# Forming A's value rows inside the first sixteen heads instead of in the lead

## The chip, the cores and the metric

The kernel runs on one core of a Trainium2 chip. Its time is the device time of one execution in microseconds (us). Before the change it was 2752.17 us, the median of three runs (2751.70 to 2752.62). The engines are TensorE (PE: matmuls, with its weight loads shown apart as PEld), VectorE (DVE), ScalarE (ACT), GpSimd (POOL) and SyncE (SP, which here only issues DMAs). Sixteen DMA engines carry all transfers, whichever queue issues them.

## The reference, cut to what matters

Two attention layers read the same `x` (2048 x 576) with 32 heads of width 18. A has its own keys and values for each head; B has one key and one value for all heads. A sigmoid gate mixes them:

```python
x = A_x
g = _sigmoid((x * gate_w).sum(-1, keepdims=True))
a = _A_ref(x, A_wqkv, A_wo)    # softmax(q k^T / sqrt(18)) v, 32 heads with own k and v, then @ wo
b = _B_ref(x, B_wq, B_wk, B_wv, B_wo)    # the same with one k and one v for 32 heads
return g * a + (1 - g) * b
```

Everything is float32. The kernel forms products of activations and weights as sums of three products of a high and a low part (h*h + l*h + h*l).

## The kernel before, in words

B's heads are units 0 to 31 (`u < H`), A's heads units 32 to 63. The program is recorded in order by hand: each engine executes its instructions in the order in which the Python code emits them, and waits come from the tiles that instructions share. There are three stages.

**The projecting stage.** `X["h"]` and `X["l"]` hold x transposed, as a high part (5 blocks of 128 rows) and a low part (4 blocks), in SBUF. All columns that are needed row-wise (B's key, gate, B's value, B's queries, A's queries and keys) are stacked into 14 tiles `mt` of 128 rows. `project(mt, c, w)` forms one quarter (512 columns) of such a tile: 14 matmuls of 512 columns (`products`, L153 of the profile) into a PSUM tile of the pool `ps_s` (three buffers, named ps). `leave` takes it out: ScalarE copies the high part into `phl` (L159; four buffers), VectorE subtracts it for the low part (L165), and a DMA on GpSimd's queue writes both to `qk_d` in DRAM. Where a tile holds keys, its second quarter also yields the difference of the first two key quarters (`pd`, `pdhl`, written to `kd_d`). Tiles 0 to 2 are done while x still arrives; `project_rest` does tiles 3 to 13, 44 quarters, one after another. Between quarters `bring_row` issues one of the loads that bring rows back for the first heads (`ksb`, `kdb`, `qs`: DMAs of 18 rows on SP's queue, which also loads weights `wst` and A's value weights `vwst`).

**The lead.** Scores are exponentiated after subtracting a row maximum, so the maxima run 22 steps ahead (`LEAD = 22`; a step is one block of 128 queries of one unit). Before the main loop, 16 slices form the first maxima. Slice `v` forms two value units, six bank products `step_max` (L412; the first two into `ps_s`, the other four into `ps_m`, which has four buffers) that VectorE reduces (L421). A value unit `project_v(st_, hf, w)` forms A's values of 128 positions for half of the heads: 14 matmuls of 288 columns (L192) into `ps_s`, a copy by ScalarE into `vst` (L195) and a DMA on ScalarE's queue to `v_d` in DRAM, from which each group of four A heads is loaded later (`load_vg`, first at step 482). At slice 11, `max_rows(0)` finishes unit 0's maxima. After the lead `open_ph2` frees X and the weights and opens the pools of the main loop.

**The main loop.** 64 units of 16 steps. A step has four score products (L447), four exponentials on ScalarE (L454), a share of later units' bank products and reduces, and the sums over values (L460). Strings of letters set the order on TensorE: s is a score product, m, x and y are bank products for the maxima, digits are quarters of sums over values, U takes one unit of side work from `todo`.

```python
PLAIN = "sm sy sm 4 sm sm sm 2 sm sx 2"
SPARSE = "sx U sm ys sx 4 sm ms sm 3 ys ms sx 3 sm ms ms 4 sm ms ms 2 ms sy 2 ms ms sx 4 ms sm ys 3 " \
         "ms ms ms 3 sm ms ms 4 sm ms"
```

PLAIN covers two steps without side work. SPARSE covers eight steps and has one U. Before the change it is used at steps 522 to 777, for the 32 units of the first output projection (`out_proj`: 12 matmuls of 288 columns into `ps_m`, L595, and a copy by ScalarE into `oacc`, L598). DENSE and ALONE serve the later parts, which the change does not touch. `when(T, f)` calls f when step T begins; `slow` is a list of generators that get one turn at each second step (gates, normalisation, output weights).

Of the kernel before, what the change touches and what calls it, by code (L numbers as in the profile page):

```python
# [8 lines left out]
F32 = mybir.dt.float32  # L9
# [33 lines left out]
def gated_mix_kernel(ctx: ExitStack, tc: tile.TileContext, xT, wall, wv, wo, out):  # L43
# [21 lines left out]
    sum_d = dram.tile([NU, S], F32, name="sum_d")  # L65
    r_d = dram.tile([NU, S], F32, name="r_d")
    v_d = dram.tile([16, P, H * 19], F32, name="v_d")
    on_d = [dram.tile([9 * P, S], F32, name=f"on{x}") for x in "hl"]


# [85 lines left out]
    def leave(mt, c, fp):  # L156
# [17 lines left out]
        if mt == 0:  # L174
            dma(z_d[cs], st[ROW_G:ROW_G + 1, :])
            return c, st

    def shared_v(c, st):
        pv = ps_m.tile([P, 512], F32, name="pm")
        for j in range(4):  # L180
            nc.tensor.transpose(pv[:, 18 * j:18 * j + 18],
                                st[ROW_VB:ROW_VB + 18, j * P:(j + 1) * P],
                                ident[ROW_VB:ROW_VB + 18, ROW_VB:ROW_VB + 18])
        nc.vector.tensor_copy(vb[:, 4 * c:4 * c + 4, 0:18],
                              pv[:, 0:72].rearrange("p (j d) -> p j d", d=18))

    vst = [stp.tile([P, 16, 19], F32, name=f"vst{i}", bufs=1) for i in range(3)]

    def project_v(st_, hf, w):
        fp = ps_s.tile([P, 512], F32, name="ps")  # L190
        for n, (a, b, k, kr) in enumerate(PROJ):
            nc.tensor.matmul(fp[:, 0:288], X[b][:kr, k, st_ * P:(st_ + 1) * P], w[a][:kr, k, :],  # L192
                             start=(n == 0), stop=(n == len(PROJ) - 1))
        t = vst[st_ % 3]
        nc.scalar.activation(t[:, :, 0:18], fp[:, 0:288].rearrange("p (h d) -> p h d", d=18), AF.Copy)  # L195
        dma(v_d[st_, :, 304 * hf:304 * hf + 304], t.rearrange("p h d -> p (h d)"), nc.scalar)

    def run(gen):
        for _ in gen:
# [9 lines left out]
        if rows_back:  # L209
            rows_back.pop(0)()  # L210

    WV = []
    VS = [None, None]
    with tc.tile_pool(name="xs", bufs=1, side="right") as xsp:
        XS = []

        def load_x(c, rest=None):
            half = c < 2
            XS.append(xsp.tile([P, NKT, 256 if half else 512], F32, name="xsh" if half else "xs", bufs=2))
            load5(XS[c], xT[:, 256 * c:256 * c + 256] if half else xT[:, 512 * (c - 1):512 * c], rest)  # L220

        def main_w(st):

            w = {y: wpool.tile([P, NKT, P], F32R, name=f"w{y}", bufs=3) for y in "hl"}
            nc.scalar.activation(w["h"][:, 0:4], st[:, 0:4], AF.Copy)
            nc.vector.tensor_tensor(w["l"][:, 0:4], st[:, 0:4], w["h"][:, 0:4].bitcast(F32), op=OP.subtract)
            return w

        def last_w(st, w):
            nc.scalar.activation(w["h"][:, 4], st[:, 4], AF.Copy)  # L230
            nc.vector.tensor_tensor(w["l"][:, 4], st[:, 4], w["h"][:, 4].bitcast(F32), op=OP.subtract)

        def split_x(c):
            xs = XS[c // 2 + 1][:, :, 256 * (c % 2):256 * (c % 2) + 256] if c > 1 else XS[c]
            cs = slice(c * 256, (c + 1) * 256)
            nc.scalar.activation(X["h"][:, :, cs], xs, AF.Copy)
            low_x(c, xs)
            last_x(c, xs)

        def low_x(c, xs):  # L240
            cs = slice(c * 256, (c + 1) * 256)
            nc.vector.tensor_tensor(X["l"][:, :, cs], xs[:, 0:4], X["h"][:, 0:4, cs].bitcast(F32), op=OP.subtract)

        def last_x(c, xs):
            xh = X["h"][64:128, 4, c * 256:(c + 1) * 256]
            nc.vector.tensor_tensor(xh, xs[64:128, 4], xh.bitcast(F32), op=OP.subtract)

        W = [load_w(0, nc.scalar)]
        load_x(0, nc.scalar)
        nc.scalar.activation(ones, ones, AF.Copy)  # L250
        W.append(load_w(1, nc.gpsimd))
        W.append(load_w(2, nc.gpsimd))
        load_x(1, nc.gpsimd)

        warm = ps_m.tile([P, 512], F32, name="pm")
        for i in range(6):
            nc.tensor.matmul(warm[:, 0:304], ident, vb.rearrange("p k d -> p (k d)"), start=True, stop=True)
        for c in range(2, 5):
            load_x(c)
        dma(ones_r.rearrange("a (b c) -> (a b) c", c=32), ones)  # L260
        for mt in range(3, 6):
            W.append(load_w(mt))
        for t in vst:
            nc.gpsimd.memset(t, 1.0)

        x0, xh = XS[0], X["h"][:, :, 0:256]
        ST = [W.pop(0) for _ in range(3)]
        WP = [main_w(ST[0])]
        nc.scalar.activation(xh[:, 0:2], x0[:, 0:2], AF.Copy)  # L269
        nc.vector.tensor_copy(xh[:, 2:4], x0[:, 2:4])  # L270
        low_x(0, x0)
        WP.append(main_w(ST[1]))
        WP.append(main_w(ST[2]))
        last_w(ST[0], WP[0])
        nc.scalar.activation(xh[:, 4], x0[:, 4], AF.Copy)
        last_x(0, x0)
        last_w(ST[1], WP[1])
        last_w(ST[2], WP[2])
        split_x(1)
        FP = [ps_s.tile([P, 512], F32, name="ps") for _ in range(3)]  # L280
        for n in ((0, 12), (12, 14)):
            for mt in range(3):
                products(FP[mt], WP[mt], 0, 0, 256, *n)
        for c in range(4):
            for mt in range(3):
                if mt == 2:
                    if c < 3:
                        split_x(2 * c + 2)
                        split_x(2 * c + 3)
                    shared_v(*keep)  # L290
                if c == 0:
                    products(FP[mt], WP[mt], 0, 256, 256)
                    done = leave(mt, c, FP[mt])
                else:
                    done = project(mt, c, WP[mt], 2 if c == 1 and mt == 0 else 1)
                if mt == 0:
                    keep = done
                    if c == 3:
                        WN = prep_w(W.pop(0))
    vwp = ph1.enter_context(tc.tile_pool(name="vwp", bufs=1, side="right"))  # L300

    def load_wv(hf):
        VS[hf] = vwp.tile([P, NKT, 288], F32, name="vwst")
        load5(VS[hf], wv[:, 288 * hf:288 * hf + 288])

    for b in (SB, MB):
        later(ksb[b + 54:b + 56, :], ones_r)
# [2 lines left out]
    for u in range(3):  # L310
        load_q(u, put=later)

    def project_rest(WN):
        for mt in range(3, MT):
            w = WN
            if mt + 1 < MT:
                WN = prep_w(W.pop(0))
            if mt + 3 < MT:
                W.append(load_w(mt + 3))
            if mt == 5:  # L320
                load_wv(0)
            for c in range(4):
                project(mt, c, w)
                bring_row()
            if mt in (8, 11):
                hf = (mt - 8) // 3
                WV.append({y: vwp.tile([P, NKT, 288], F32R, name=f"vw{y}{hf}") for y in "hl"})
                split_w(VS[hf], WV[hf], nc.vector)
                if hf == 0:
                    load_wv(1)  # L330
        assert not rows_back

    project_rest(WN)


    small = ctx.enter_context(tc.tile_pool(name="small", bufs=1, side="left"))
# [32 lines left out]
    def open_ph2():  # L369
        ph1.close()  # L370
        L["pt"] = ctx.enter_context(tc.tile_pool(name="ppool", bufs=14, side="left"))
        L["work"] = ctx.enter_context(tc.tile_pool(name="work", bufs=2, side="left"))
        p2 = ctx.enter_context(tc.tile_pool(name="p2", bufs=1, side="right"))
        L["pool"] = p2
        L["ks"] = [p2.tile([P, S], F32R, name=f"ksa{i}") for i in range(2)] + [ksb]
        L["kds"] = [p2.tile([P, 512], F32R, name="kda"), kdb]
        L["oacc"] = p2.tile([P, 16, D], F32, name="oacc")
        for t in L["ks"][:2]:
            for b in (SB, MB):
                dma(t[b + 54:b + 56, :], ones_r)  # L380

    VG = {}

# [319 lines left out]
    for t in range(8):  # L703
        when(16 * (last_head(t) + 1) + 5, lambda t=t: slow.append(normalise(t)))
    when(16 * (NU - 1) + 2, lambda: run(normalise(8, at_end=True)))
    SEG = ((0, [P] * 4, 450, 518), (4, [P] * 4, 862, 942))
    for t0, rows, Ta, Tb in SEG:
        when(Ta, lambda t0=t0, rows=rows: slow.append(prep_wo(t0, rows)))
# [2 lines left out]
    when(980, load_gates)  # L711


    vunits = [(st_, hf) for hf in range(2) for st_ in range(16)]
    banks = [(M, c) for M in range(LEAD + 2) for c in range(4)]
    for v in range(16):
        if v == 11:
            max_rows(0)
        for st_, hf in vunits[2 * v:2 * v + 2]:
            project_v(st_, hf, WV[hf])  # L720
        for n, (M, c) in enumerate(banks[6 * v:6 * v + 6]):
            step_max(*divmod(M, 16), c, c % 2 == 1, ps_s if n < 2 else ps_m)
        if v >= 4 and slow:
# [64 lines left out]
    while pos["s"] < 4 * NSTEP:  # L788
# [4 lines left out]
            emit(ALONE, 1 if T < 1012 else 0)  # L793
        elif T >= SEG[1][3] + 4:
            emit(DENSE, 1)
        elif SEG[0][3] + 4 <= T < SEG[0][3] + 4 + 8 * 32:
            emit(SPARSE, 1)
        else:
            emit(PLAIN)
# [43 lines left out]
```

## Time and profile before

| what | us |
|---|---|
| median of three runs | 2752.17 |
| the profiled execution, its own time | 2752.82 |
| its span, first to last instruction | 2750.5 |
| TensorE busy | 2741.8 |
| VectorE busy | 2413.1 |
| ScalarE busy | 2432.6 |
| GpSimd busy | 216.8 |
| the lead, from the first value matmul to the first score | 189.85 to 266.37 |

The mean granted clock of TensorE was 0.999. The profile comes as a page (busy times, the span in slices, DMA queues, the chain of work that ended last, the costliest groups of instructions) and as answers from the trace: the chain in order of time, a timeline of single instructions, busy times by stretch, DMA landings. Rows of a timeline give the start, the length, the engine, the line, the operation, what is written and read, the shapes, and how many instructions were merged; a bracket says how long the engine was idle before and who ended that. A matmul's length is modelled and overlaps its successor, so the pace is read from starts. In rows of stretches the columns are busy time of TensorE, weight loads, VectorE, ScalarE and GpSimd with their counts, then the granted clock, the share of the DMA engines and GB/s.

### The profile page before, as it was taken

How to read it: one execution, taken by the hardware profiler on the slowest of the kernel's cores; microseconds unless marked ns; L12 is line 12 of the kernel's file. 1: busy time of each engine (PE TensorE's matmuls, PEld its weight loads, DVE VectorE, ACT ScalarE, POOL GpSimd, SP SyncE). 2: the span in 40 equal slices, each digit the busy share in tenths (PEclk: the TensorE clock that was granted, in tenths of full speed). 3: DMA queues.
4: the chain of work that ended last, by engine and by line, in shares of the span. 5: the costliest groups of instructions: out<-in, count | busy, mean ns of one | idle time of the engine just before them, and what ended most of it. 6: DMA issues, size and time to landing. Idle time of an engine off the chain costs nothing.

```text
span 2750.5 us, 59178 instructions
## 1 busy us (share of the span) xinstructions
PE 2741.8 (100%) x22968; PEld 1264.3 (46%) x22968; DVE 2413.1 (88%) x4521; ACT 2432.6 (88%) x4781; POOL 216.8 (8%) x355
## 2 busy tenths in 40 slices
PE   9999999999999999999999999999999999999999
PEld 7888333333333333333334444444444333334554
DVE  4347999999999999999999898898989999998873
ACT  4322999999999999999999999999999999998776
POOL 2220000001000100100110001000100011011000
PEclk9999999999999999999999999999999999999999
DMA  8752010112102111210133223222321233223312
GB/s 283 271 222 70 25 32 27 33 47 67 31 27 56 52 32 35 63 47 27 53 94 107 84 60 94 93 68 74 102 86 47 67 88 96 67 81 116 111 35 88
DMA packets 123511, 217.24 MB, mean 79 GB/s; under 512 B 53082, under 2 KB 80810, under 8 KB 111544
## 3 DMA queue, kind: packets, MB, share of 16 engines
q1 hardware_dynamic: 107806, 170.79, 20.8%
q0 software_dynamic: 10496, 37.49, 3.6%
q10 hardware_dynamic: 4928, 5.18, 0.5%
q8 instruction: 180, 2.95, 0.5%
q14 instruction: 101, 0.83, 0.1%
HBM read 137.23 MB, written 67.40 MB: 74 GB/s over the span
## 4 chain that ended last, share of the span: by engine, by line
PE 98%; DVE 1%; DMA 1%; SPq 0%; ACT 0%; issue 0%; DVEq 0%; ACTq 0%
PE acc L460 38%; PE ps L447 36%; PE pm L412 9%; PE ps L153 6%; PE pm L595 4%; PE ps L192 2%; DVE mx L421 1%; DMA xsh<-xT 0%; PE pm L447 0%; PE ps L412 0%; DMA R<-r_d 0%; DMA r_d<-sm 0%; SPq L49 0%; DVE oacc L604 0%; DVE junk L418 0%
## 5 line engine op out<-in xcount | busy, mean ns | idle before, releaser
L454 ACT ACTIVATE pt<-ps 128x512 f32<-128x512 f32 x4052 | 2129.9, 611 | 106.6 <-PE pm L412 44.6
L421 DVE TENSOR_REDUCE mx<-pm 128x1 f32<-128x512 f32 x3064 | 1945.7, 683 | 140.3 <-PE pm L412 96.3
L447 PE MATMUL ps<-qs,ksb 56*128 56x512 f32 x2688 | 905.8, 437 | 0.3
L412 PE MATMUL pm<-ksb,qs 54*128 54x512 f32 x2332 | 807.0, 441 | 0.0
L447 PEld LDWEIGHTS ps<-qs,ksb 56*128 56x128 f32 x2688 | 437.2, 184 | 643.1 <-ACT pt L454 618.1
L460 PE MATMUL acc<-pt,vb 128*19 128x256 f32 (+1 forms) x6144 | 592.5, 457 | 0.1
L460 PE MATMUL acc<-pt,vg 128*19 128x256 f32 (+3 forms) x6432 | 573.8, 443 | 0.4 <-DVE oe L472 0.4
L447 PE MATMUL ps<-qs,ksa 56*128 56x512 f32 x1364 | 453.7, 437 | 0.1
L412 PE MATMUL pm<-ksa,qs 54*128 54x512 f32 x1232 | 425.5, 438 | 0.0
L412 PEld LDWEIGHTS pm<-ksb,qs 54*128 54x128 f32 x2332 | 373.8, 184 | 35.1 <-DVE mx L421 15.2
L418 DVE CUSTOM_DVE_ANT_0 junk<-pm,xb 128x512 bf16<-128x512 f32 x500 | 339.7, 679 | 1.0 <-ACT xb L415 0.9
L447 PEld LDWEIGHTS ps<-qs,ksa 56*128 56x128 f32 x1364 | 218.0, 184 | 246.7 <-ACT pt L454 217.6
L415 ACT ACTIVATE xb<-pm 128x512 f32<-128x512 f32 x500 | 305.2, 610 | 0.0
L412 PEld LDWEIGHTS pm<-ksa,qs 54*128 54x128 f32 x1232 | 197.7, 184 | 56.5 <-DVE mx L421 26.0
L460 PEld LDWEIGHTS acc<-pt,vg 128*19 128x19 f32 x6432 | 122.1, 97 | 215.3 <-issue 190.0
L460 PEld LDWEIGHTS acc<-pt,vb 128*19 128x19 f32 x6144 | 104.2, 97 | 210.3 <-issue 200.2
L412 PE MATMUL pm<-kdb,qs 54*128 54x512 f32 x372 | 150.4, 404 | 0.0
L115 POOL CAST mh<-mt 128x32 fp32r<-128x32 f32 x64 | 13.5, 211 | 1726.0 <-DVE mt L429 1725.9
L159 ACT ACTIVATE phl<-ps 128x512 fp32r<-128x512 f32 x56 | 33.5, 599 | 100.8 <-PE ps L153 72.0
L165 DVE TENSOR_TENSOR phl<-ps,phl 128x512 fp32r<-128x512 f32 x56 | 38.7, 691 | 92.0 <-ACT phl L159 69.4
L153 PE MATMUL ps<-xh,wh 128*128 128x512 f32 (+1 forms) x300 | 83.5, 377 | 0.6 <-ACT xh L269 0.6
L153 PE MATMUL ps<-xh,wl 128*128 128x512 f32 (+1 forms) x300 | 83.2, 375 | 0.0
(123 smaller groups left out, 1379.6 us busy)
## 6 DMA issues: line engine op xcount, KB each, us to landing
qs<-qk SPq DMA_DIRECT2D x384, 144.0 KB
qk<-phl POOLq DMA_DIRECT2D x56, 512.0 KB, 4.6
ksa<-qk SPq DMA_DIRECT2D x132, 144.0 KB
ksb<-qk SPq DMA_DIRECT2D x66, 144.0 KB
onh<-oh SPq DMA_DIRECT2D x32, 256.0 KB
onl<-ol SPq DMA_DIRECT2D x32, 256.0 KB
oih<-onh SPq DMA_DIRECT2D x16, 512.0 KB
oil<-onl SPq DMA_DIRECT2D x16, 512.0 KB
```

The costliest lines, as they stand in the source:

```text
L153: nc.tensor.matmul(fp[:, p0:p0 + g], w[a][:kr, k, :], X[b][:kr, k, x0 + p0:x0 + p0 + g], start=(n == 0), stop=(n == len(PROJ) - 1))
L159: nc.scalar.activation(hl[:, 0, :], fp, AF.Copy)
L165: nc.vector.tensor_tensor(hl[:, 1, :], fp, hl[:, 0, :].bitcast(F32), op=OP.subtract)
L192: nc.tensor.matmul(fp[:, 0:288], X[b][:kr, k, st_ * P:(st_ + 1) * P], w[a][:kr, k, :], start=(n == 0), stop=(n == len(PROJ) - 1))
L412: nc.tensor.matmul(pm, qs[u % 3][b:b + 54, i * P:(i + 1) * P], k, start=True, stop=True)
L415: nc.scalar.activation(MX["x", u, i], pm, AF.Relu)
L418: nc.vector.tensor_tensor_reduce(junk, pm, MX.pop(("x", u, i)), 1.0, -3e38, op0=OP.add, op1=OP.max, accum_out=MX[u][:, i, c:c + 1])
L421: nc.vector.tensor_reduce(MX[u][:, i, c:c + 1], pm, axis=AX.X, op=OP.max)
L447: nc.tensor.matmul(ps, kst(u)[b:b + 56, i * P:(i + 1) * P], qs[u % 3][b:b + 56, c * 512:(c + 1) * 512], start=True, stop=True)
L454: nc.scalar.activation(pt, ps, AF.Exp, scale=SCALE)
L460: nc.tensor.matmul(acc[32 * j:32 * j + 19, a:b], v_of(u, i), PT[u, i, j][:, a:b], start=(i == 0), stop=(i == 15), skip_group_check=True)
L595: nc.tensor.matmul(fp[:, 0:288], x, y, start=(n == 0 and not joins), stop=(n == len(ops) - 1))
```

## The change

Three things move.

1. The value units leave the lead. They become a generator `value_units`, whose 32 units are taken one for each SPARSE block of eight steps at steps 10 to 265, in heads 0 to 16. A unit has the same 14 matmuls and the same copy, but into `ps_m`, and its result is stored from SP's queue.
2. By then X has been freed, so its parts go through DRAM: in the projecting stage eight stores (`store_x`, after every third quarter) write X to `x_d`, and the split value weights go to `wv_d` in four stores (`store_wv`), all on GpSimd's queue. The value weights are loaded from the first quarter on, and one set of split buffers serves both halves. In the main loop `value_units` loads the four weight parts once and, for every two units, the 128 columns of X (`xv`, two buffers) on SP's queue. The rows that were brought back over 44 quarters are brought back over 28.
3. The last four tiles of projected rows, mt 10 to 13 (16 quarters), are formed in the lead, one per slice, in place of the two value units. They leave through `leave_lead`: ScalarE copies the PSUM tile twice (plain, and high part), and GpSimd subtracts, in place of VectorE.

The accumulator `oacc` gets its memory after the value units are done (`open_oacc`, step 274).

```diff
+    x_d = dram.tile([P, 2 * NKT - 1, S], F32, name="x_d")
+    wv_d = dram.tile([2, 2, P, NKT * 288], F32, name="wv_d")
...
+    def leave_lead(mt, c, fp):
+        hl = stp.tile([P, 2, 512], F32R, name="phl", bufs=4)
+        st = stp.tile([P, 512], F32, name="pst", bufs=3)
+        nc.scalar.activation(st, fp, AF.Copy)
+        nc.scalar.activation(hl[:, 0, :], fp, AF.Copy)
+        nc.gpsimd.tensor_tensor(hl[:, 1, :], st, hl[:, 0, :].bitcast(F32), op=OP.subtract)
+        dma(qk_d[:, mt * P:(mt + 1) * P, c * 512:(c + 1) * 512].rearrange("a p f -> p a f"), hl, nc.gpsimd)
+        if c == 0:
+            KD[mt] = st
+        if c == 1:
+            d = stp.tile([P, 512], F32, name="pd", bufs=1)
+            nc.gpsimd.tensor_tensor(d, st, KD.pop(mt), op=OP.subtract)
+            dhl = stp.tile([P, 2, 512], F32R, name="pdhl", bufs=1)
+            split(d, dhl[:, 0, :], dhl[:, 1, :], nc.scalar, nc.gpsimd)
+            dma(kd_d[mt * P:(mt + 1) * P, 0:2, :], dhl, nc.gpsimd)
+            dma(kd_d[mt * P:(mt + 1) * P, 2, :], dhl[:, 0, :], nc.gpsimd)
...
+    def store_wv(hf, st):
+        w = {y: vwp.tile([P, NKT, 288], F32R, name=f"vw{y}") for y in "hl"}
+        split_w(st, w, nc.vector)
+        for i, y in enumerate("hl"):
+            dma(wv_d[hf, i], w[y].rearrange("p k f -> p (k f)"), nc.gpsimd)
+
+    def store_x(i):
+        y, c = "hl"[i % 2], i // 2
+        cs = slice(512 * c, 512 * c + 512)
+        dma(x_d[:, 0:NKT, cs] if y == "h" else x_d[:, NKT:, cs], X[y][:, :, cs], nc.gpsimd)
...
+    left = tiles_left(WN)
+    for n in range(4 * (LEAD_T - 3)):
+        mt, c, w = next(left)
+        if n in (0, 10):
+            vs = load_wv(n // 10)
+        project(mt, c, w)
+        bring_row()
+        if c == 3:
+            bring_row()
+        if n in (8, 18):
+            store_wv(n // 10, vs)
+        if n % 3 == 1 and n // 3 < 8:
+            store_x(n // 3)
...
+    def value_units():
+        pool = L["vx"]
+        XV = {}
+        def load(st_):
+            XV[st_] = pool.tile([P, 2 * NKT - 1, P], F32R, name="xv", bufs=2)
+            dma(XV[st_], x_d[:, :, st_ * P:(st_ + 1) * P])
+        load(0)
...
+        yield
+        for st_ in range(16):
+            if st_ < 15:
+                load(st_ + 1)
+            x = XV.pop(st_)
+            for hf in range(2):
+                fp = ps_m.tile([P, 512], F32, name="pm")
+                for n, (a, b, k, kr) in enumerate(PROJ):
+                    nc.tensor.matmul(fp[:, 0:288], x[:kr, k if b == "h" else NKT + k, :], w[hf][a][:kr, k, :],
+                                     start=(n == 0), stop=(n == len(PROJ) - 1))
+                nc.scalar.activation(vst[hf][:, :, 0:18], fp[:, 0:288].rearrange("p (h d) -> p h d", d=18), AF.Copy)
+                dma(v_d[st_, :, 304 * hf:304 * hf + 304], vst[hf].rearrange("p h d -> p (h d)"))
+                yield
...
+    VB = 10
+    when(VB - 8, lambda: (todo.append(value_units()), pull(1)))
+    when(VB + 8 * 32 + 8, open_oacc)
...
-        for st_, hf in vunits[2 * v:2 * v + 2]:
-            project_v(st_, hf, WV[hf])
+        mt, c, w = next(left)
+        fp = ps_s.tile([P, 512], F32, name="ps")
+        products(fp, w, c * 512, 0, 512)
+        leave_lead(mt, c, fp)
...
-        elif SEG[0][3] + 4 <= T < SEG[0][3] + 4 + 8 * 32:
+        elif any(b <= T < b + 8 * 32 for b in (VB, SEG[0][3] + 4)):
             emit(SPARSE, 1)
```

`tiles_left` yields (mt, c, w) for tiles 3 to 13 in the order of `project_rest`, with the same weight loads and splits ahead. Here `LEAD_T` is `MT - 4`, so the loop above forms 28 quarters and the lead the other 16.

More of the change, by code (lines that the diff above doesn't have):

```diff
@@ L185, in shared_v @@
                               pv[:, 0:72].rearrange("p (j d) -> p j d", d=18))
[L187 to L196, printed above, removed]
     def run(gen):
@@ L210, in bring_row @@
             rows_back.pop(0)()
-    WV = []
-    VS = [None, None]
     with tc.tile_pool(name="xs", bufs=1, side="right") as xsp:
@@ L262, in gated_mix_kernel @@
             W.append(load_w(mt))
-        for t in vst:
-            nc.gpsimd.memset(t, 1.0)
         x0, xh = XS[0], X["h"][:, :, 0:256]
@@ L302, in load_wv @@
     def load_wv(hf):
-        VS[hf] = vwp.tile([P, NKT, 288], F32, name="vwst")
-        load5(VS[hf], wv[:, 288 * hf:288 * hf + 288])
+        t = vwp.tile([P, NKT, 288], F32, name="vwst")
+        load5(t, wv[:, 288 * hf:288 * hf + 288])
+        return t
+    def store_wv(hf, st):
[7 more added lines that the diff above has]
+        dma(x_d[:, 0:NKT, cs] if y == "h" else x_d[:, NKT:, cs], X[y][:, :, cs], nc.gpsimd)
     for b in (SB, MB):
@@ L311, in gated_mix_kernel, with tiles_left @@
         load_q(u, put=later)
-    def project_rest(WN):
+    LEAD_T = MT - 4
+    def tiles_left(WN):
         for mt in range(3, MT):
@@ L319, in project_rest @@
                 W.append(load_w(mt + 3))
-            if mt == 5:
-                load_wv(0)
             for c in range(4):
[L323 to L333, printed above, removed]
+                yield mt, c, w
+    left = tiles_left(WN)
[11 more added lines that the diff above has]
+            store_x(n // 3)
+    assert not rows_back
     small = ctx.enter_context(tc.tile_pool(name="small", bufs=1, side="left"))
@@ L376, in open_ph2 @@
         L["kds"] = [p2.tile([P, 512], F32R, name="kda"), kdb]
-        L["oacc"] = p2.tile([P, 16, D], F32, name="oacc")
+        L["early"] = ExitStack()
+        L["vx"] = L["early"].enter_context(tc.tile_pool(name="vx", bufs=1, side="right"))
         for t in L["ks"][:2]:
@@ L380, in open_ph2, with open_oacc @@
                 dma(t[b + 54:b + 56, :], ones_r)
+    def open_oacc():
+        L["early"].close()
+        L["oacc"] = ctx.enter_context(tc.tile_pool(name="oacc", bufs=1, side="right")) \
+            .tile([P, 16, D], F32, name="oacc")
+    def value_units():
[5 more added lines that the diff above has]
+        load(0)
+        w = [{y: pool.tile([P, NKT, 288], F32R, name=f"vw{y}{hf}") for y in "hl"} for hf in range(2)]
+        for hf in range(2):
+            for i, y in enumerate("hl"):
+                dma(w[hf][y], wv_d[hf, i].rearrange("p (k f) -> p k f", k=NKT))
+        vst = [pool.tile([P, 16, 19], F32, name=f"vst{i}") for i in range(2)]
+        for t in vst:
+            nc.gpsimd.memset(t, 1.0)
+        yield
[3 more added lines that the diff above has]
+            x = XV.pop(st_)
+            for hf in range(2):
+                fp = ps_m.tile([P, 512], F32, name="pm")
[5 more added lines that the diff above has]
+                yield
     VG = {}
@@ L711, in gated_mix_kernel @@
     when(980, load_gates)
-    vunits = [(st_, hf) for hf in range(2) for st_ in range(16)]
     banks = [(M, c) for M in range(LEAD + 2) for c in range(4)]
```

## The prediction

> **What bounds the kernel now.** I read the page first (busy time, the chain that ended last), then the chain in order of time, then single stretches.
>
> ```profile
> PE 2741.8 (100%) x22968; PEld 1264.3 (46%) x22968; DVE 2413.1 (88%) x4521; ACT 2432.6 (88%) x4781; POOL 216.8 (8%) x355
> ...
> PE 98%; DVE 1%; DMA 1%; SPq 0%; ACT 0%; issue 0%; DVEq 0%; ACTq 0%
> ```
>
> TensorE is busy all the time and carries 98% of the chain. The change removes no matmul; it moves matmuls between three stretches, so its worth is the difference of what they cost there, plus whatever new wait makes TensorE stop. The chain in order of time gives the price in each:
>
> ```profile
> 46.96 143.05 PE ps L153 x630
> 190.01 3.71 PE ps L192 x28
> ...
> 261.73 3.90 PE ps L192 x28
> ...
> 311.20 1.05 PE acc L460 x8
> 348.23 1.05 PE acc L460 x8
> ...
> 1478.42 1.78 PE pm L595 x12
> ...
> 2093.59 1.79 PE pm L595 x12
> ```
>
> Columns are start, length, what, and how many matmuls. The projecting stage runs 630 matmuls, 45 tiles of 14, in 143.05 us: 3.179 us a tile. The lead's slices follow each other every (261.73 - 190.01) / 15 = 4.78 us. A head of 16 plain steps takes 348.23 - 311.20 = 37.03 us, so 8 steps 18.52. Eight steps with one unit of the first output projection, the SPARSE pattern, take (2093.59 - 1478.42) / 31 = 19.84.
>
> **The change, part by part.**
>
> *Tiles out of the projecting stage.* Sixteen leave: 16 x 3.179 = 50.9 us saved, all on the path.
>
> *Value units into heads 0 to 16.* A projection unit has 12 matmuls of 288 columns, a value unit 14.
>
> ```profile
> 1577.55 0.79 PE L595 MATMUL pm<-woh,oih 128*128 128x288 f32 x4
> ...
> 1578.19 0.69 PE L595 MATMUL pm<-woh,oil 128*128 128x288 f32 x4
> ...
> 1578.72 0.69 PE L595 MATMUL pm<-wol,oih 128*128 128x288 f32 x4
> ...
> 1579.34 0.18 PEld L447 LDWEIGHTS ps<-qs,ksa 56*128 56x128 f32 x1 [0.16 <-ACT xb L415]
> ```
>
> Four start 0.53 us apart, so one takes 0.133. A unit of 12 costs 19.84 - 18.52 = 1.33 us over plain steps (the SPARSE order returns part of it), one of 14 costs 1.59. 32 x 1.59 = 51.0 us added. The other engines do not bind there:
>
> ```profile
> 311.00:348.00 37.00, 37.00 (x322) 14.05 (x320) 35.58 (x68) 36.33 (x73) 0.47 (x2) 1.00 0.11 31
> ...
> 1478.40:1637.20 158.80, 158.80 (x1506) 77.26 (x1505) 140.75 (x267) 149.63 (x295) 1.86 (x8) 1.00 0.25 75
> ```
>
> Columns: TensorE, weight loads, VectorE, ScalarE, GpSimd, granted clock, DMA share, GB/s. ScalarE falls from 98% in plain steps to 94% beside units; the value unit's eviction (128x288) has the shape of the projection unit's. The loads of X parts, 576 KB every 16 steps, and the stores of 152 KB, now on SP's queue instead of ACT's, meet a DMA share of 0.11: nothing. What stands behind the store on SP are row loads for two or three heads ahead, nothing that a 2 us wait makes late. If the cover were gone, each late load would stop TensorE for its own landing.
>
> *Start of the units.* Xv and four weight parts, 576 + 4 x 720 KB = 3.5 MB, are issued after the lead and needed at step 10, some 22 us after it. At 315 GB/s (SP's rate, below) they take 11 us, after up to 7 us for the last writes of the lead whose memory they take. Cost 0; late at most 3 us.
>
> *The lead.* Products move from 28 matmuls of 288 columns a slice to 14 of 512.
>
> ```profile
> 256.87 0.79 PE L192 MATMUL ps<-vwh,xh 128*128 128x288 f32 x4
> ...
> 260.55 0.29 PE L192 MATMUL ps<-vwl,xh 128*128 128x288 f32 x1
> 260.77 0.50 PE L412 MATMUL ps<-ksb,qs 54*128 54x512 f32 x2
> ...
> 261.31 1.29 DVE L421 TENSOR_REDUCE mx<-ps 128x1 f32<-128x512 f32 x2 [1.12 <-PE ps L412]
> ...
> 261.67 0.80 PE L192 MATMUL ps<-vwh,xh 128*128 128x288 f32 x4
> ```
>
> ```profile
> L117 POOL TENSOR_TENSOR ol<-ot,oh 128x512 fp32r<-128x512 f32 x32 | 41.2, 1286 | 6.9 <-DMA onl<-ol 4.9
> ...
> L49 POOL DMA_DIRECT2D qk<-phl x56 | 40.6, 726 | 123.2 <-DVE phl L165 117.5 <-issue 3.6 <-DVE vb L184 2.0
> ...
> L159 ACT ACTIVATE phl<-ps 128x512 fp32r<-128x512 f32 x56 | 33.5, 599 | 100.8 <-PE ps L153 72.0 <-issue 26.6 <-ACT wh L125 1.3
> ...
> L421 DVE TENSOR_REDUCE mx<-ps 128x1 f32<-128x512 f32 x32 | 20.6, 686 | 18.9 <-PE ps L412 18.9
> ...
> L126 DVE TENSOR_TENSOR wl<-wst,wh 128x640 fp32r<-128x640 f32 x11 | 9.1, 825 | 0.0
> L125 ACT ACTIVATE wh<-wst 128x640 fp32r<-128x640 f32 x11 | 8.0, 731 | 0.0
> ```
>
> These are groups: count | busy us, mean ns of one | idle before. Products take 260.77 - 256.87 = 3.90 us, 28 x 0.133 = 3.71 of it streaming and 0.19 the switch; the six bank products 0.90. With TensorE alone the new slice is 3.18 + 0.19 + 0.90 = 4.27. But three tiles a slice now come out of the three buffers ps where there were four, and in the built order the products of most slices take the buffer that the first bank product of the slice before held. Its reduce starts at 261.31, 0.54 after the product, and lasts 0.69; with 0.16 for TensorE to go on, as after xb in the rows of the unit, it resumes 1.39 after the first bank product, not 0.90. Slice: 3.18 + 0.19 + 1.39 = 4.76, sixteen of them 0.3 us below before. Where a slice takes the buffer of the products before it, ScalarE's two copies are waited for, and at c = 1 ScalarE itself waits for GpSimd (subtract, issue, subtract). Two copies of 0.60 delay three slices by some 0.35 us; 2 x 1.29 + 0.73 = 3.3 us before the split at c = 1 delays one by 0.9: together +2. GpSimd's own load, six subtractions and six issues or 12 us in four slices of 19, is hidden; so are three weight splits that come along (0.73 on ScalarE, 0.83 on VectorE, which has 4.76 - 6 x 0.69 = 0.6 to spare a slice). Lead: +1.7, between -8.2 (all slices 4.27) and +5 (ScalarE's copies waited for in each).
>
> *New traffic in the projecting stage.* This is the term that decides. X goes out in eight stores (1280 or 1024 KB), the split value weights in four of 720 KB, all on GpSimd's queue between the writes of projected rows.
>
> ```profile
> q0 software_dynamic: 8415, 30.42, 56.1%
> q1 hardware_dynamic: 4506, 7.52, 16.7%
> ...
> qk<-phl POOLq DMA_DIRECT2D x45, 512.0 KB, 4.3
> kd<-pdhl POOLq DMA_DIRECT2D x9, 512.0 KB, 4.0
> ...
> kd<-pdhl POOLq DMA_DIRECT2D x9, 256.0 KB, 4.1
> ```
>
> These are the DMA view's rows for 47 to 190 us: packets, MB, share of 16 engines; then issues with KB and us to landing. GpSimd's queue moves 30.42 MB in 56.1% of 143 us, 379 GB/s of full share; SP's 7.52 MB in 16.7%, 315 GB/s. In the 22 tiles from the first X store to the last (69.9 us of TensorE), the new queue holds 22 x 512 + 4 x 768 + 9216 + 2880 KB = 27.1 MB, SP's 22/28 of 7.52 = 5.9 MB. At those rates that is 71.4 + 18.8 = 90.2 us of all engines. The densest stretch shows how far the engines go:
>
> ```profile
> 28.00:40.00 12.00, 12.00 (x56) 9.68 (x55) 7.19 (x10) 6.01 (x8) 3.36 (x5) 1.00 1.04 403
> 60.00:80.00 20.00, 20.00 (x90) 16.57 (x89) 5.68 (x8) 5.80 (x10) 4.35 (x6) 1.00 0.93 327
> 95.00:120.00 25.00, 25.00 (x112) 20.71 (x111) 9.63 (x14) 8.19 (x14) 8.03 (x12) 1.00 0.61 231
> ```
>
> ```profile
> DMA to landing us min/median/max: 7.2/8.0/8.3
> ```
>
> ```profile
> DMA to landing us min/median/max: 3.1/3.2/4.9
> ```
>
> The last two are the landings of qk writes issued from 60 to 80 us and from 95 to 120, where SP's queue is empty.
>
> The share reaches 1.04 for 12 us, so 90.2 / 1.04 = 86.7 us: 16.8 more than TensorE needs. Some of it is hidden. Each tile's copy waits for the write four tiles earlier (phl has four buffers), issued 1.7 us after that tile, so 4 x 3.18 - 1.6 = 11.1 us may pass; three PSUM buffers let TensorE run on for 4.9 more. A landing may take 16 us before TensorE stops. From 60 to 80 us, where SP's row loads run beside the writes, it already takes 8.0. So 8 us are left and 16.8 - 8 = 8.8 us of stall remain. Ends: at the 403 GB/s of the first row 33.0 MB take 81.9 us, a stall of 4.0; with neither the 1.04 nor any slack 20.3. I take 8.8, since the row with both queues at work measures the same loads. A store of 640 pieces is issued by GpSimd in 0.73 us or a few times that, beside some 2 us of idle time a tile.
>
> The Trainium skill, HBM Reference, Specifications, says a core streaming alone reaches about 425 GB/s; by that 33.0 MB would take 77.6 us and the slack would hide all of the excess, an estimate. The rows here reach 403.
>
> **Sum:** -50.9 + 51.0 + 1.7 + 8.8 = +10.6 us. The profiled execution took 2752.82 us, 0.65 over the median 2752.17; against the median: 2762.8.
>
> A stop long enough also costs clock:
>
> ```profile
> 265.00:270.00 5.00, 4.70 (x19) 2.47 (x18) 3.68 (x6) 3.62 (x8) 0.00 (x0) 0.91 0.20 70
> 270.00:275.00 5.00, 5.00 (x20) 2.21 (x21) 2.12 (x5) 3.16 (x8) 0.00 (x0) 0.50 0.02 7
> 275.00:280.00 5.00, 5.00 (x40) 1.56 (x38) 4.36 (x8) 4.46 (x9) 0.00 (x0) 0.91 0.00 0
> ```
>
> Where scores wait for exponentials the granted clock falls to 0.50; (0.09 + 0.50 + 0.09) x 5 = 3.4 us of clock are lost. In a stretch bound by transfers that is free, at its end it may add up to 3.4.
>
> **The rivals.**
>
> 1. *Transfers keep up* (not slower). Place: the 22 tiles. It decides from 33.0 MB / (69.9 + 8) = 424 GB/s on. For: 403 was held beside small loads, and the stores are large. Against: landings of 8.0 us at a share of 0.93. Time: 2762.8 - 8.8 = 2754.
> 2. *The lead runs at TensorE's pace*, 4.27 a slice: -8.2 in place of +1.7. For: VectorE has time to spare in each slice. Against: the buffer order. Time: 2753 with the stall, 2744 where rival 1 holds too, the one way to be faster by over 0.2%.
> 3. *The stall is longer*: no slack, 20.3 us, a cold clock at its end (+3.4). For: SP's loads of 18 rows come closer together, and lengthened landings from 3.2 to 8.0. Time: 2762.8 + 11.5 + 3.4 = 2778.
>
> **How the numbers follow.** Forecast 0.50, own range 2758 to 2770. Rival 1 alone 0.18, rival 2 with the stall 0.08, both together 0.08, rival 3 0.16. The range leaves out half of rival 3 and rivals 1 and 2 together: 2748 to 2775. Within 0.2% of 2752.17 (2746.7 to 2757.7, about what a measurement of this kernel can tell from no change) lie rival 1 but for 0.03 with lead slices in between, rival 2 with the stall, and 0.03 of the forecast's with a stall near 4: 0.15 + 0.08 + 0.03 = 0.26. Faster: 0.08 + 0.03 = 0.11. Slower: 0.47 + 0.16 = 0.63.
>
> **What would show it.** Right: in the profile after, the projecting stage's 28 later tiles take about 98 us instead of 89, with ScalarE's copies into phl waiting for DMA, the share of the engines near 1.0 and landings of 12 to 17 us; lead slices of 4.7 to 4.8 us whose products wait for VectorE's reduce; heads 0 to 16 at 20.1 us per 8 steps. Wrong: no TensorE gap before the lead; lead slices near 4.3; a gap at the first unit; or units that cost under 1.3 or over 1.9 us.

## The result and the profile after

The changed kernel takes 2762.76 us (median of six runs, 2761.49 to 2763.48), the kernel before in the same runs 2752.11: a ratio of 1.0039, 95% interval 1.0026 to 1.0052. The prediction was 2762.8. The profiled execution of the changed kernel took 2762.81 us with a span of 2761.0, against 2752.82 and 2750.5 before.

First the page of the changed kernel: busy time, and the engines' shares of the chain that ended last.

```profile
PE 2738.1 (99%) x23480; PEld 1296.8 (47%) x23480; DVE 2394.6 (87%) x4497; ACT 2443.7 (89%) x4793; POOL 256.7 (9%) x390
...
PE 96%; DMA 2%; DVE 1%; ACT 0%; issue 0%; POOL 0%; ACTq 0%; POOLq 0%
```

TensorE's share of the chain fell from 98% to 96%; that of transfers rose from 1% to 2%, and the chain has a row that it did not have before, the writes of projected rows (`DMA qk<-phl`, 1.6%). The chain in order of time (start, length, what, how many) shows where they are:

```profile
47.47 31.99 PE ps L155 x140
...
94.34 15.19 DMA qk<-phl
...
113.35 15.79 DMA qk<-phl
...
129.67 14.14 DMA qk<-phl
...
164.90 3.44 PE ps L155 x14
...
220.79 3.44 PE ps L155 x14
...
250.55 2.04 PE pm L437 x14
...
873.59 2.08 PE pm L437 x14
```

The projecting stage, an unbroken row of matmuls before, now hangs three times on the landing of a write of projected rows. The slices of the lead follow each other every (220.79 - 164.90) / 12 = 4.66 us, and the value units (L437) every (873.59 - 250.55) / 31 = 20.10 us. TensorE's timeline of the projecting stage has three stops (idle time before, and who ended it, in brackets):

```profile
107.63 0.39 PE L155 MATMUL ps<-xh,wl 128*128 128x512 f32 x1
108.60 1.20 PE L155 MATMUL ps<-xh,wh 128*128 128x512 f32 x4 [0.59 <-DVE phl L167]
...
118.03 0.39 PE L155 MATMUL ps<-xh,wl 128*128 128x512 f32 x1
122.38 2.07 PE L155 MATMUL ps<-xh,wh 128*128 128x512 f32 x4 [3.97 <-DVE phl L167]
124.25 1.91 PE L155 MATMUL ps<-xh,wl 128*128 128x512 f32 x4
...
128.25 1.08 PE L155 MATMUL ps<-xh,wh 128*128 128x512 f32 x4
...
143.91 0.39 PE L155 MATMUL ps<-xh,wl 128*128 128x512 f32 x1
145.78 1.21 PE L155 MATMUL ps<-xh,wh 128*128 128x512 f32 x4 [1.49 <-DVE phl L167]
...
149.13 1.07 PE L155 MATMUL ps<-xh,wh 128*128 128x512 f32 x4
```

The row at 149.13 is the first product of the lead. The stops are named after VectorE, which frees the PSUM buffer, but VectorE waits for ScalarE's copy, and that copy for a write. The chain of waits from 47 to 150 us (us in total, times, longest) and the landings of the writes issued from 90 to 105 and from 105 to 120 us say so:

```profile
DVE phl L167 <- ACT phl L161: 51.6, 21, 6.4
...
ACT phl L161 <- DMA qk<-phl: 30.5, 12, 6.5
```

```profile
DMA to landing us min/median/max: 14.6/15.8/18.6
```

```profile
DMA to landing us min/median/max: 12.8/13.8/15.8
```

And the stretches of the stage (TensorE, weight loads, VectorE, ScalarE, GpSimd, granted clock, DMA share, GB/s):

```profile
100.00:110.00 10.00, 9.41 (x42) 7.48 (x41) 2.15 (x4) 2.19 (x4) 3.48 (x5) 1.00 1.02 380
110.00:120.00 10.00, 8.41 (x38) 6.63 (x36) 2.67 (x4) 1.96 (x4) 3.32 (x5) 1.00 1.02 388
120.00:130.00 10.00, 7.62 (x22) 6.09 (x23) 4.41 (x6) 4.69 (x7) 3.77 (x6) 0.66 1.01 368
130.00:140.00 10.00, 10.00 (x46) 8.29 (x45) 2.62 (x5) 1.94 (x4) 3.56 (x6) 1.00 1.04 410
```

The DMA engines are full (1.01 to 1.04) at 368 to 410 GB/s. From 120 to 130 us the clock was 0.66: after the stop of 3.97 us one quarter took 128.25 - 122.38 = 5.87 us instead of 3.18.

The balance of the two profiled executions:

| stretch | before, us | after, us | change | predicted |
|---|---|---|---|---|
| start to the projecting stage | 46.96 | 47.47 | +0.5 | 0 |
| projecting stage, 45 and 29 quarters | 142.9 | 101.66 | -41.2 | -50.9 + 8.8 = -42.1 |
| lead | 76.5 | 76.3 | -0.2 | +1.7 |
| first score to the end | 2484.1 | 2535.6 | +51.4 | +51.0 |
| span | 2750.5 | 2761.0 | +10.5 | +10.6 |

The 142.9 runs to the start of the first value matmul at 189.85; the 143.05 of the chain's row overlaps it a little. 29 quarters at 3.179 us are 92.2 us, so 9.5 us of the 101.66 are the stall.

### The profile page after: what moved, and what is told of

Read it like the earlier page. It is cut to its first block, busy times and chain, and to the rows that moved or that the text cites. A ratio compares the mean times of both kernels' runs of the same rounds, so it can differ in the third digit from the quotient of the medians.

```text
span 2761.0 us, 60302 instructions
## 1 busy us (share of the span) xinstructions
PE 2738.1 (99%) x23480; PEld 1296.8 (47%) x23480; DVE 2394.6 (87%) x4497; ACT 2443.7 (89%) x4793; POOL 256.7 (9%) x390
## 4 chain that ended last, share of the span: by engine, by line
PE 96%; DMA 2%; DVE 1%; ACT 0%; issue 0%; POOL 0%; ACTq 0%; POOLq 0%
PE acc L521 38%; PE ps L508 32%; PE pm L473 14%; PE pm L656 4%; PE ps L155 4%; PE pm L437 2%; DMA qk<-phl 2%; DVE mx L482 0%; DMA xsh<-xT 0%; PE pm L508 0%; PE ps L473 0%; DVE oacc L665 0%; DMA wst<-wall 0%; DVE phl L167 0%; ACT phl L185 0%
## 5 line engine op out<-in xcount | busy, mean ns | idle before, releaser
L473 PE MATMUL pm<-ksb,qs 54*128 54x512 f32 x2332 | 791.5, 437 | 0.0
L521 PE MATMUL acc<-pt,vb 128*19 128x256 f32 (+3 forms) x6656 | 580.2, 434 | 0.1
L521 PEld LDWEIGHTS acc<-pt,vb 128*19 128x19 f32 x6656 | 125.4, 97 | 216.8 <-issue 193.3
L161 ACT ACTIVATE phl<-ps 128x512 fp32r<-128x512 f32 x40 | 23.9, 598 | 82.1 <-PE ps L155 46.8
L167 DVE TENSOR_TENSOR phl<-ps,phl 128x512 fp32r<-128x512 f32 x40 | 27.7, 691 | 73.5 <-ACT phl L161 57.5
```

Of the source, the lines that this page charges most:

```text
L161: nc.scalar.activation(hl[:, 0, :], fp, AF.Copy)
L167: nc.vector.tensor_tensor(hl[:, 1, :], fp, hl[:, 0, :].bitcast(F32), op=OP.subtract)
L473: nc.tensor.matmul(pm, qs[u % 3][b:b + 54, i * P:(i + 1) * P], k, start=True, stop=True)
L521: nc.tensor.matmul(acc[32 * j:32 * j + 19, a:b], v_of(u, i), PT[u, i, j][:, a:b], start=(i == 0), stop=(i == 15), skip_group_check=True)
```

## The experiments

The theory: the additional 10.6 us are the stall, the stall is the bytes of the added stores over the rate of the engines, and the moved work itself nearly cancels. Besides each time I give the start of the first value unit, read as above from the chain in order of time (250.55 in the changed kernel): behind it every kernel below takes 2510.2 to 2511.2 us in its profiled execution, so a difference at this point is a difference of the time. The projecting stage itself starts at 46.3 to 47.5 us in these executions, so about 1 us of such a difference can come from ahead of it.

**The X stores in the lead.** The same eight stores, one in each of the first eight slices of the lead instead of the projecting stage.

```diff
-        if n % 3 == 1 and n // 3 < 8:
-            store_x(n // 3)
...
         leave_lead(mt, c, fp)
+        if v < 8:
+            store_x(v)
```

> The eight X stores go out in the first eight lead slices (where the DMA share is 0.4 to 0.5) instead of in the projecting stage; the weight stores stay. Theory (the added traffic fills the engines in the projecting stage, 9.5 us of stall): the stage's TensorE gaps go, the time falls by 8 to 10 us to 2753 to 2755, lead slices stay at 4.66 us. Rival (the row loads that come closer together make the stall): it keeps half of it or more, 2757 or above.

Measured: 2751.02 us, 0.9996 of the kernel before (0.9987 to 1.0006); the first unit starts at 238.88, 11.7 us earlier. The stall is gone, by more than it was costed at: the time is 2 us below the lower end that was expected. The stretch of the stage, the wait of the copies from 47 to 150 us, and a slice of the lead:

```profile
100.00:120.00 20.00, 20.00 (x90) 16.58 (x89) 8.62 (x11) 7.74 (x12) 7.03 (x11) 1.00 0.97 357
```

```profile
ACT phl L161 <- DMA qk<-phl: 6.4, 2, 5.8
```

```profile
148.40 1.20 PE L155 MATMUL ps<-xh,wh 128*128 128x512 f32 x4 [0.32 <-DVE mx L480]
```

The copies wait 6.4 us in place of 30.5, and TensorE does not stop in the stage. The lead has room for the stores: its slices stay at 4.67 us. So the 11.7 are the stall of 9.5, 0.5 by which the changed kernel's stage began later (47.47 against 47.00), and 1.7 in the first two slices of its lead (5.61 and 5.52). The first of these follows the last late copy out of the stage, so it is lateness carried over. In the second a bank product stood 1.17 us for ScalarE's copies, which had waited for no write; with six buffers (below) that stop is there too, behind a first slice of 4.58, so it is not shown to come from the stage.

**More bytes.** Each X store is issued a second time, in one kernel to the same place, in a later one to a DRAM tensor of its own.

```diff
+        dma(x_d[:, 0:NKT, cs] if y == "h" else x_d[:, NKT:, cs], X[y][:, :, cs], nc.gpsimd)
```

> Each X store is issued twice in a row, 9.44 MB more in the projecting stage. Theory (bytes over the engines' rate, the slack is already spent): 9.44 MB at 403 GB/s are 23.4 us, less what the last six tiles can still take up: +20 to +23, 2782 to 2786. Rival (the stall comes from the place of single stores in the queue, not from bytes): under +12, 2775 or less.

Measured: 2812.41 us, 1.0219 (1.0205 to 1.0233), about twice the loss that was expected. The waits from 60 to 180 us say why it tells nothing of bytes:

```profile
POOL x_d L49 <- DMA x_d<-xh: 52.3, 5, 14.4
...
POOL x_d L49 <- DMA x_d<-xl: 27.2, 2, 18.1
```

The second store waited for the landing of the first, which it overwrites, and GpSimd's queue stood behind it. Without that wait:

```diff
+    x2_d = dram.tile([P, 2 * NKT - 1, S], F32, name="x2_d")
...
+        dma(x2_d[:, 0:NKT, cs] if y == "h" else x2_d[:, NKT:, cs], X[y][:, :, cs], nc.gpsimd)
```

> Each X store is issued twice again, the second time to a DRAM tensor of its own, so that no store waits for another store's landing. Theory (the stall is bytes over the engines' rate): 9.44 MB more at the 410 GB/s that the changed kernel held in this stage are 23.0 us, all of them stall: 2762.8 + 23.0 = 2786, between 2783 and 2790 with what cold clock adds; no long waits of GpSimd's queue for x_d, a share of the engines near 1.0 throughout. Rival (each large store costs a wait of its own, whatever its bytes): twelve stores made 9.5 us, 0.8 each, so eight more make 6.3: 2769.

Measured: 2788.39 us, 1.0134 (1.0117 to 1.0150); the first unit starts at 276.79, 26.2 us later. GpSimd's waits for these landings ahead of an x_d store fell to 5.4 and 3.5 us in all (60 to 180 us).

```profile
100.00:120.00 20.00, 11.52 (x42) 8.35 (x40) 2.67 (x4) 1.82 (x3) 5.03 (x7) 0.91 1.02 376
120.00:140.00 20.00, 12.89 (x45) 10.15 (x46) 5.46 (x8) 6.11 (x10) 6.51 (x10) 0.78 1.03 403
```

9.44 MB more cost 25.6 us, at a full share: 368 GB/s at the margin, with what the low clock of these rows (0.91 and 0.78) adds. Bytes over rate stands (23.0 by 410 GB/s, 25.6 measured), eight waits of 0.8 us each do not.

**Earlier room: fewer loads in the stage.** Twelve loads of rows for units 1 and 2 (each 144 KB) are recorded in the lead, one per slice, instead of in the projecting stage.

```diff
-    for u in range(3):
-        load_q(u, put=later)
+    load_q(0, put=later)
...
+    for u in (1, 2):
+        load_q(u, put=later)
...
         leave_lead(mt, c, fp)
+        bring_row()
```

> The twelve row loads for units 1 and 2 (144 KB each, 1.77 MB) move from the projecting stage into the lead, one per slice. Theory (all bytes count by their queue's rate): 1.77 MB at 315 GB/s and a share of 1.04 are 5.4 us less, 2757 to 2758. Rival that SP's loads weigh more, because they burden some engines: the stall goes, 2753 to 2755. Rival that they do not matter: 2762.

Measured: 2760.13 us, 1.0031 (1.0019 to 1.0043), 2.6 us less than the changed kernel where more was expected. Its longest stop, with slow matmuls behind it, and the loads of query rows (`qs`) as SP issued them from 114 to 209 us:

```profile
137.90 2.08 PE L155 MATMUL ps<-xh,wh 128*128 128x512 f32 x4 [3.26 <-DVE phl L167]
```

```profile
114.52 7.79 SPq L49 DMA_DIRECT2D qs<-qk  x5
...
124.09 4.65 SPq L49 DMA_DIRECT2D qs<-qk  x3
...
184.69 0.72 SPq L49 DMA_DIRECT2D qs<-qk  x1
...
187.54 1.49 SPq L49 DMA_DIRECT2D qs<-qk  x2
...
208.66 0.77 SPq L49 DMA_DIRECT2D qs<-qk  x1
```

The edit did not do what was meant. The lead starts at 146.08 in this execution, and the six loads of unit 0 were out by 92 us, so these rows are the twelve: eight of them still went out inside the stage, and only four in the lead. SP is ordered by its own instructions and by the tiles it waits for, and it ran ahead of the place in the program. Four loads are 0.59 MB, an estimated 1.6 us at the 368 GB/s above; 2.6 were measured, with run-to-run ranges of some 2 us, so the run agrees with bytes over rate and does not test it sharply. What all twelve would give stays open.

**More buffers.** `phl` with six and with five buffers instead of four, which should let the engines be late by one or two tiles more.

```diff
-        hl = stp.tile([P, 2, 512], F32R, name="phl", bufs=4)
+        hl = stp.tile([P, 2, 512], F32R, name="phl", bufs=6)
```

> phl has six buffers instead of four. Theory (TensorE stops once a landing takes longer than the buffers last, 3.18 us for each): 6.4 us more slack, stall 9.5 to some 3 us, 2756 to 2757. Rival (something else, the buffers of pdhl or of PSUM, stops it first): 2760 to 2763.

Measured: 2763.96 us, 1.0044 (1.0029 to 1.0059). No gain in all, though the stage became 2.9 us shorter (46.83 to the lead's first product at 145.55, 98.7 us against 101.66). The first waits below are from 90 to 150 us; the other two rows are the start of the main loop, first TensorE's timeline, then the waits from 220 to 232 us.

```profile
ACT pdhl L115 <- DMA kd<-pdhl: 23.3, 4, 9.6
```

```profile
227.14 2.76 PE L508 MATMUL ps<-qs,ksb 56*128 56x512 f32 x5 [5.16 <-ACT pt L515]
```

```profile
ACT pt L515 <- DMA qk<-phl: 5.6, 1, 5.6
```

In the stage ScalarE now waited for the single buffer of `pdhl`, which kept the gain below the 6.4 us expected. The main loop lost it again: the larger `phl` lay where the main loop has its exponentials, and TensorE, three scores in, stood 5.16 us until the last writes of rows had left that memory. Five buffers avoid this overlap.

> Five phl buffers instead of four; the memory of the fifth lies outside what the main loop's first exponentials take. Theory (the slack term: each buffer lets the engines be late by one tile more): 3.2 us less, 2759.6, with the first scores on time. Rival (the wait only moves to the single buffer of pdhl, as with six): 2762 to 2763.

Measured: 2762.50 us, 1.0039 (1.0025 to 1.0053); first unit at 250.17. The stage did become 3.1 us shorter (46.33 to the lead's first product at 144.90, 98.6 us against 101.66), as the theory had it, but the lead gave it back in its first two slices. The last row below is the wait behind the stop at 151.79 (144 to 165 us):

```profile
132.85 1.19 PE L155 MATMUL ps<-xh,wh 128*128 128x512 f32 x4 [2.21 <-DVE phl L167]
...
144.90 1.17 PE L155 MATMUL ps<-xh,wh 128*128 128x512 f32 x4 [1.04 <-DVE pd L171]
...
151.79 1.94 PE L155 MATMUL ps<-xh,wh 128*128 128x512 f32 x4 [2.14 <-ACT phl L185]
```

```profile
ACT phl L185 <- DMA qk<-phl: 2.1, 1, 2.1
```

Its copies go into the same buffers, behind the same writes. The stop of 2.14 us also cost clock: the 14 matmuls behind it took 4.9 us instead of 3.18. The rival's time came true, but the stage did gain as the theory said; it was lost in the lead. Buffers move the wait, and where the backlog of writes reaches into a next stage with the same buffers, little of it is gained.

**Another queue.** All twelve stores on SP's queue instead of GpSimd's.

```diff
-            dma(wv_d[hf, i], w[y].rearrange("p k f -> p (k f)"), nc.gpsimd)
+            dma(wv_d[hf, i], w[y].rearrange("p k f -> p (k f)"))
...
-        dma(x_d[:, 0:NKT, cs] if y == "h" else x_d[:, NKT:, cs], X[y][:, :, cs], nc.gpsimd)
+        dma(x_d[:, 0:NKT, cs] if y == "h" else x_d[:, NKT:, cs], X[y][:, :, cs])
```

> The same stores at the same places, issued on SP's queue instead of GpSimd's. Theory (the engines' total rate): the bytes are the same, so what the projected rows gain the row loads lose; the waits move to the lead's first bank products, 2758 to 2763. Rival (the writes of projected rows stand behind the stores in one queue): without that the stall goes, 2753 to 2755.

Measured: 2767.98 us, 1.0058 (1.0041 to 1.0075), worse than the changed kernel by 5.2 us, and neither forecast. A stretch of the stage, the one stop, and the wait behind it (140 to 180 us):

```profile
100.00:120.00 20.00, 20.00 (x90) 16.55 (x89) 8.50 (x11) 7.75 (x12) 5.85 (x9) 1.00 1.01 379
```

```profile
158.40 2.07 PE L155 MATMUL ps<-xh,wh 128*128 128x512 f32 x4 [15.12 <-ACT phl L185]
```

```profile
ACT wh L127 <- DMA wst<-wall: 15.3, 1, 15.3
```

TensorE did not stop in the stage at all, with the same bytes; it stopped once, 15.12 us, in the lead. ScalarE stood for a weight tile that it had to split and whose load was behind the stores on SP's queue, and the copies that free TensorE's PSUM buffers come after that split in ScalarE's order. The engines' rate sets how much is late; the queue that holds the stores decides what is late.

**The lead's slices.** In `leave_lead` the high part is copied from the plain copy in SBUF, not a second time from PSUM, so that the PSUM buffer is free one copy earlier. First in the changed kernel, then together with the X stores in the lead.

```diff
-        nc.scalar.activation(hl[:, 0, :], fp, AF.Copy)
+        nc.scalar.activation(hl[:, 0, :], st, AF.Copy)
```

> In the lead the high part is copied from the plain copy in SBUF instead of from PSUM, so PSUM is free after the first of ScalarE's two copies; in the built order all products then take one buffer and wait for that copy. Theory (the slice of 4.66 us is the wait for the PSUM buffer, its reduce on VectorE): slices near 4.3, -5 to -6 us in all, 2757. Rival (VectorE's six reduces or GpSimd bind): slices stay above 4.55, 2761 or more.

Measured: 2761.28 us, 1.0034 (1.0022 to 1.0046), 1.5 us less in place of almost 6. Most slices took 4.28 us, but every fourth 5.5 to 5.7:

```profile
184.03 1.20 PE L155 MATMUL ps<-xh,wh 128*128 128x512 f32 x4 [1.32 <-ACT pst L184]
...
202.31 1.20 PE L155 MATMUL ps<-xh,wh 128*128 128x512 f32 x4 [1.10 <-ACT pst L184]
```

> X stores in the lead and one copy from PSUM together. Theory: both gains add, 2762.8 - 9 - 5.5 = 2748, some 4 us under the kernel before the change. Rival (the stores' issue on GpSimd delays the subtractions and so the buffers in the lead): 2752 or more.

Measured: 2750.55 us, 0.9995 (0.9986 to 1.0004), not below before. In `one_copy` each slow slice follows one with c = 1, whose copy into `pdhl` makes ScalarE wait for GpSimd's difference (15.0 us in four waits, 150 to 225 us), with the next tile's copy behind it. With the X stores in the lead the four waits are 16.2 us (140 to 215), and the slow slices are less regular. That copy went to GpSimd next:

```diff
-            split(d, dhl[:, 0, :], dhl[:, 1, :], nc.scalar, nc.gpsimd)
+            split(d, dhl[:, 0, :], dhl[:, 1, :], nc.gpsimd, nc.gpsimd)
```

> X stores in the lead and the high part copied from SBUF, as in x_lead_one_copy, and at c = 1 the difference's high part is copied by GpSimd instead of ScalarE, so that ScalarE never waits for GpSimd. Theory (that wait is what keeps every fourth slice at 5.5): all slices near 4.3, some 1.2 us less in each of four: 2750.6 - 4 to 5 = 2746, between 2745 and 2748, below the kernel before by 0.2%. Rival (VectorE's reduces hold the slices in any case): 2750.

Measured: 2748.25 us, 0.9986 (0.9977 to 0.9996). The slices (from bank product to bank product) are 4.27 us up to the eighth, then 5.03, 5.62 and 4.93, where GpSimd is behind: 17.92 of 20 us busy. VectorE, which has little to spare in a slice, stood 2.96 us for a step of the gate that GpSimd formed late, and its next reduces came late for it:

```profile
160.00:180.00 20.00, 19.12 (x86) 12.98 (x83) 15.90 (x27) 6.47 (x13) 17.92 (x21) 1.00 1.01 365
```

```profile
175.09 0.35 DVE L368 RECIPROCAL g<-g 128x32 f32<-128x32 f32 x1 [2.96 <-POOL g L366]
```

Last, the stores in slices without a difference (`XAT = (0, 2, 3, 4, 6, 7, 8, 10)`):

```diff
-        if v < 8:
-            store_x(v)
+        if v in XAT:
+            store_x(XAT.index(v))
```

> As x_lead_gps, but the eight X stores lie in slices 0, 2, 3, 4, 6, 7, 8 and 10, where GpSimd has no difference to form. Theory (in x_lead_gps GpSimd is behind from the second slice to the eighth and the slices 8 to 10 take 5.0, 5.6 and 4.9 us for it): all slices 4.28, 2.8 us less: 2748.2 - 2.8 = 2745.5, between 2744.5 and 2747. Rival (the DMA engines, at a share of 1.01 from 160 to 180 us, make these slices late whatever GpSimd does): 2748.

Measured: 2746.95 us, 0.9981 (0.9972 to 0.9990): 5 us below the kernel before, 15.8 below the change. It lies within the expected bounds, at their upper end. The chain in order of time has slices of 156.39 - 152.12 = 4.27:

```profile
152.12 3.38 PE ps L156 x14
...
156.39 3.38 PE ps L156 x14
```

Three later slices still took 5.03, 4.63 and 4.67: VectorE's wait for the gate is 1.30 us there instead of 2.96, and these slices are 1.25 us shorter together, less than half of the 2.8 expected. The first scores came at 0.83 of the clock (205 to 225 us; 0.91 in the run ahead), so in the profile it is no faster than the one ahead of it (spans 2745.7 and 2745.3). Whether spreading the stores itself gains anything is open: the intervals overlap.

## Why the prediction was right

*Tiles out of the projecting stage, -50.9; value units in the heads, +51.0.* Both right. A unit's block takes 20.10 us (predicted 18.52 + 1.59 = 20.11), and the main loop is 51.4 longer. No late start: the first unit came without a stop.

*New traffic, +8.8.* Right in place, chain and size: 9.5 us, with a share of 1.01 to 1.04, ScalarE's copies waiting for writes, landings of 12.8 to 18.6 us. Moving the eight stores away takes 11.7 us off, adding their bytes again puts 25.6 on. Two parts of its working were off and made up for each other. Counted from start to start (one matmul takes 0.23 us), the stops are 0.7 + 4.1 + 1.6 = 6.5 us, a little more than the brackets 0.59, 3.97 and 1.49 say, since a matmul's modelled length overlaps its successor. 2.7 are the low clock that the step kept for rival 3 ((1 - 0.66) x 10 = 3.4, of which 5.87 - 3.18 = 2.7 lay in a quarter on the path), and 0.3 lie in the quarters behind the two other stops (3.31 and 3.35 us): 9.5. So the waiting alone was below the 8.8, and the clock filled it up. And the 8 us of slack were counted as gained for good. The run with five buffers shows that slack can be only lent: the backlog went into the lead and was paid there. In the changed kernel about 1 us of the lead's first slice was paid so.

*The lead, +1.7.* The mechanism was right (the products of most slices wait some 0.3 us for VectorE's reduce), the sizes were not: slices of 4.66 instead of 4.76, and of the 2 us for ScalarE's copies at most 0.9 appeared, in the second slice; three later slices wait 0.28 for them, no longer than others wait for the reduce. With the stores in the lead it takes 74.6 us (213.72 - 139.1) from its first product to the first score, 1.9 below before; so without the X stores in the stage the term is -1.9, where +1.7 was forecast. The changed kernel's 76.3 holds the 1.7 us of its first two slices on top.

*The rivals.* Rival 1, transfers that keep up, needed 424 GB/s; the best 10 us had 410. The Trainium skill, HBM Reference, Specifications, gives about 425 GB/s for a core that streams alone; no stretch of 10 us here reached it, so the measured 410 decides. Rival 2, a lead at TensorE's pace of 4.27, is a mechanism that is there, but not in the change: with the copy from SBUF most slices reached 4.28, with GpSimd's cast nearly all 4.27. Rival 3's low clock appeared, its longer stall did not.

The sum came out to 0.1 us, its terms (start, projecting stage, lead, main loop) to 0.5, 0.9, 1.9 and 0.4: that they cancel so well is luck.

## What to carry to other kernels

Cost an added store by the stretch it lands in: bytes over the rate that the engines hold there when full, less the slack of the buffers, and count slack as gained only if the transfers catch up before the next stage uses the same buffers. Then look for a stretch whose engines are idle: the same stores cost 11.7 us in the projecting stage and nothing in the lead right behind it. When moving a large transfer to another queue, read what stands behind it there; it is that which will be late. When moving a load to a later place in the program, read from the trace when its queue issued it.

## What the runs showed of the hardware

- A stop of TensorE costs more than itself. Behind the stops of 3.97 and 3.26 us the first four matmuls took 2.07 to 2.08 us instead of 1.2, and the quarter behind 3.97 took 5.87 instead of 3.18, at a granted clock of 0.50 from 122 to 126 us; behind stops of 0.59 and 1.49 us a quarter took 3.31 and 3.35. Between, it goes either way: 2.14 us with five buffers was followed by 1.94, and a stop of 2.21 in the same run by 1.19. With each X store issued twice to one place a stop of 2.81 us was followed by 2.05, and behind one of 3.98 the first four still took 1.16 and only the next four 1.78. The Trainium skill, TensorE: Matmul & The Clock Gate, Part 1, has the clock halved after an idle window of some 3.4 us that runs free of the kernel; the halving agrees, the slow starts after 2.14 and 2.81 us of idle time do not fit a whole idle window.
- At a full share (1.01 to 1.04) the DMA engines of the changed kernel moved between 343 (80 to 90 us) and 410 GB/s (130 to 140) in 10 us; a share of 1.0 is not one rate.
- A second store to the same place in DRAM waited up to 18.1 us for the landing of the first, and with it all that GpSimd had to issue behind it; to a tensor of its own it did not. This is the order that the program keeps between writes to one tensor.
